# Attention beside a gated feed-forward on one core: the opening reordered, the last even head normalized by transfers, and quarters of output pieces in score bursts

## The chip, the cores and the metric

The kernel runs on one core of one Trainium2 chip. The metric is device time in microseconds (us), from launch to end. The kernel before took 656.79 us (median of three runs, 656.19 to 660.07).

## The reference, cut to what matters

Two branches read the same input `x` (2048 rows of 512) and are mixed row by row with a sigmoid gate. The attention has 32 heads of only 16 columns; the feed-forward has 1376 inner columns and no nonlinearity.

```python
def _A_ref(x, wqkv, wo):                      # H = 32, Dh = 16
    qkv = (x @ wqkv).reshape(B, S, 3, H, Dh).transpose(2, 0, 3, 1, 4)
    scores = einsum("bhqd,bhkd->bhqk", q, k) * (Dh ** -0.5)
    o = einsum("bhqk,bhkd->bhqd", softmax(scores), v)
    return o.transpose(0, 2, 1, 3).reshape(B, S, D) @ wo
def _B_ref(x, w_gate, w_up, w_down):
    return ((x @ w_gate) * (x @ w_up)) @ w_down
g = sigmoid((x * gate_w).sum(-1, keepdims=True))
return g * _A_ref(x, wqkv, wo) + (1 - g) * _B_ref(x, w_gate, w_up, w_down)
```

## The kernel before, in words

**A planner writes the program.** While the kernel is built, a small simulation with an assumed duration for every operation decides the order of the instructions on each engine. Whenever an engine is free and more than one step is possible, `choose` takes the step that the next digit of the string `ORDER` names. What comes out is a fixed list of instructions for each engine, each with the semaphores that it waits for. The assumed durations and latencies (`lat=`, the numbers behind each task, `MM`, `SWITCH`) therefore never run on the chip; they only steer the order.

**Scores.** The queries are cut into 4 chunks of 512 and the heads into 4 blocks of 8, even and odd heads apart: 32 groups. A group has 64 units; a unit is the scores of one head for 128 keys and 512 queries, one matmul (L907) that uses 32 of the 128 rows of the TensorE array. Up to four units, one for each row tile of 32, are issued together as a burst (`burst`). Each unit fills one PSUM bank. There are eight banks: one (`OB`) collects the attention output, and the other seven are shared by score units and by fills.

**Exponentials.** ScalarE takes one or two banks at a time (L968); VectorE takes others with an integer trick (L1002), and GpSimd makes two shifted copies of those (L1051). The products with V (L1100) follow, four column tiles of 32 to a pass.

**Fills.** Everything else on TensorE is a "tile" of four or more pieces, each a pass of four column-tile matmuls (L427): projections `q`, `k`, `v`, the gate `z`, up and gate columns `u` and `g`, and 16 output tiles `o`. An output tile has 15 pieces: 11 with `wd` and the feed-forward's inner result `hT`, and 4 with `wo` and the attention output `OT`. An open tile holds one PSUM bank until its last piece has run.

**Quarters.** The kernel before already holds code by which a burst of fewer than four units takes along a quarter of a fill piece in an empty row tile: 32 of the piece's 128 contraction rows, accumulated into the bank of the tile that the piece belongs to. It is switched off by `Q_KINDS = ""`:

```python
def quarter(js):                              # js: row tiles that the burst's units use
    if len(js) > 3 or not Q_KINDS:
        return None
    tl = parted()                             # a tile one of whose pieces is begun in quarters
    if tl is not None:
        q = next((q for q in tl.quart if q not in js), None)
        return None if q is None else (tl, tl.part, q)
    ...                                       # else the last ready piece of an open tile
```

A piece that is begun in quarters needs all four, one in each row tile, and each quarter waits for the one before it. While its tile has no whole piece left to run, `plan_burst` keeps the row tile of the next quarter free of units (`force`).

**Normalization.** When a group's products are done, VectorE copies them to `oc` (L1192); row 16 (even) or 14 (odd) of each 32 holds the sum of the exponentials. For a pair of groups, transfers bring the sums to `dn` (L1183), VectorE takes reciprocals and multiplies by the gate (L1182, L1180), transfers take the result through DRAM to `rb` (L1179, L1175), and VectorE multiplies `oc` by `rb` into `OT` (L1173). The last pair, groups 30 and 31, goes another way: a float32 matmul with the selector `sel` spreads the sums over the partitions (L1212 for group 30, L1219 for group 31, into one bank), the gate is loaded into `rb` for itself (`tail_even`, L1199), and VectorE does the reciprocals in four parts (L1229, L1232).

**Opening.** Four loads bring the first 512 rows of `x`; TensorE transposes them (L463, copied out by L473 on ScalarE and L475 on VectorE). Matmuls on zeros (L388) fill TensorE before and after. The other rows come by twelve transposing transfers on SyncE's queue. Weights are loaded on SyncE's and ScalarE's queues.

Of the kernel before, what the change touches and what calls it, by code (L numbers as in the profile page):

```python
# [10 lines left out]
F32 = mybir.dt.float32  # L11
I16 = mybir.dt.int16
I32 = mybir.dt.int32
I64 = mybir.dt.int64
# [189 lines left out]
def bass_gated_mix__mha_block__glu_gated_bilinear__prompt_kernel(  # L204
# [15 lines left out]
    "0000000000000001000100000000000000000000100001000000000000202000000024000001000001000000010000100000"  # L220
    "0100003000000001010000000120000200010100000300000100010001000000001010000400000000200000001000500000"
    "0000010000034020100000000000000050000000001000000000120401100000000000000000000000000000000000001011"
    "1000000400000000010000000020000020000300000000000030000000000000000000000000000003000000000000000000"
    "0000200000001000000000100002000000001002100211000001000000200000001000000002000000100000000000000200"
    "0000000000000100000010000002000000000001100011000100000000000100000000000000000000100000050000400000"
    "0000010000000000001010012020000000010000000000000100000000010200000000001102020000000001010000000100"
    "0000000000000000400000000000000000100001000010001000000000001000001000000000000001000000002000000101"
    "1000010000003001000010040000000000000004010000010000101004100000000000000000000001000010100120010000"
    "0000010000000000100400000000000000000001000301000001000000000000050000000100000000000000000000000000"
    "4001010100030000010100002010100000002000000000001000010040000000000000001000000000010100000000000000"  # L230
    "0000000000000000000000000100100000000000000001010001000000000000100001000100000000000000000000001010"
    "0000000000001100000000000000010000020000000000001010101000001000100100041301000001002000000002001000"
    "0000000010000000000040000000001000000000000010000000000000001000000000020000000000000040000011000000"
    "0001000000001000000000001000010000000000200000010000400000010000100000000000000000100000000000000000"
    "0001000000000001000000001000001000000000000000000000100010000014001000000101000000000000000000000000"
    "0000001000010200001000000001000002000000050000000000010210000000020100001000002300000000400004000000"
    "0040000100000000000000000000000000000000000500000000000000000000000004000001100000200000101000000001"
    "0000000000000100010010000000000000000000000000020000200000000000000100000020000000110000100100000001"
    "0000005000000004010000000021010001004000000000020000000000000000000000000000010000000000000000010000"
    "1002000000002000103000000003001000000000400000100200000000000000000010050000000020000000000100000000"  # L240
    "1000001000000004000000000000000000000000000000101000001000001000015000000002000000000130200000010000"
    "0000000000010100000000000000400000001000001000010200000000000000000000001000000001001000100000001010"
    "0000100000020010000100200000004000000000001000100010000000101000020000020000010000400000000000000012"
    "0040000000100030000100000100000040000000000000000010000000000000000000000000000000000050000000000000"
    "0000000000004000001000000000001000000000100100010000010000002000000000100030010000000000001000000400"
    "1000000000001000000001000002000000000000000000000000000000000010000000010010000000000001000000000000"
    "0000000011000000000000000000000000101000000000000001100100000000100000000004010000000010000010000000"
    "0000000100000050000000010010000000200000000000000001010000000011000010020000140010010000000110104000"
    "0000000000120000004000010000040000000000000010000005000000000000002000020000000000000000000000001100"
    "000000000000000000000010000010010000000000000000000000000000000000000"  # L250
# [12 lines left out]
MM, SWITCH, SECOND, MML = 216.0, 106.0, 10.0, 390.0  # L263
# [26 lines left out]
def _build(nc, A_x, A_wqkv, A_wo, W_gate, W_up, W_down, gate_w, out):  # L290
# [8 lines left out]
    with ExitStack() as stack:  # L299
# [32 lines left out]
        sel = sb("sel", [128, 2, 128], F32)  # L332
# [24 lines left out]
        for t in range(4):  # L357
            load(("sp", "act")[t % 2], f"x0{t}", xr[:, t, :], x2[t * 128 : (t + 1) * 128, :], lat=3600)
        load("sp", "wq0", wq[:, :, 0:128], wcol(0, 128), lat=3600)
        load("act", "wk0", wk[:, :, 0:128], wcol(D, D + 128), lat=3600)  # L360
        load("act", "wv", wv, wcol(2 * D, 3 * D), lat=5000)
        t_x = {}
        for ch in range(1, NCH):
            for kt in range(KD):
                load("sp", f"x{ch}{kt}", xT[:, kt, ch * 512 : (ch + 1) * 512],
                     x2[ch * 512 : (ch + 1) * 512, kt * 128 : (kt + 1) * 128], lat=3500, transpose=True)
                K.tasks["sp"][-1][4] = 1330.0
        load("act", "gw", gw[:, :], gate_w.rearrange("(kt p) -> p kt", p=128), lat=6000, prio=7, allow_slow_non_contiguous=True)
        load("act", "wk1", wk[:, :, 128:D], wcol(D + 128, 2 * D), lat=9000, prio=7)
        load("act", "wq1", wq[:, :, 128:D], wcol(128, D), lat=11000, prio=7)  # L370
# [15 lines left out]
        for i in range(11):  # L386
            K.task("pe", lambda: [c["pt0"]] if "pt0" in c else None,
                   lambda pe: pe.matmul(ps[:, OB, :], PT[:, 0, 0:128], PT[:, 0, :], start=True, stop=True), 427.0, 630.0, None, 0,  # L388
                   begun=lambda o: pt_first.append(o), gate=(lambda: not any(tl.name[0] == "x" for tl in tiles)) if i > 8 else None)
# [13 lines left out]
        const("dve", "sl", lambda v: v.memset(sel[:, :, :], -1.0))  # L403
        for j in range(4):
            for p in range(2):
                const("dve", f"sl{j}{p}", lambda v, j=j, p=p: v.memset(sel[:, p, 32 * j + 16 * p : 32 * j + 16 * p + 16], 32.0 * j + 17 - 2 * p), ["sl"], 70, 120)
        const("dve", "sel", lambda v: v.tensor_scalar(sel[:, :, :], sel[:, :, :], io[:, 289:290], None, ALU.is_equal),
              [f"sl{j}{p}" for j in range(4) for p in range(2)] + ["io3"], 330, 400)
# [3 lines left out]
        const("dve", "qz0", lambda v: v.memset(QE[:, :, 1:NB, :], 0.0), (), 1340, 1400)  # L412
# [713 lines left out]
        def finish(m, last):  # L1126
# [8 lines left out]
            def done(o):  # L1135
# [49 lines left out]
                if m == NG - 2:  # L1185
                    tail_even(o)
                if m == NG - 1:
                    tail_odd(last, o)
# [411 lines left out]
```

## Time and profile before

| | |
|---|---|
| median of 3 runs | 656.79 us (656.19 to 660.07) |
| profiled execution | 657.3 us, of which the span from first to last instruction is 655.4 us |
| TensorE matmul busy | 648.9 us (99%) in 8704 matmuls |
| ScalarE busy | 630.3 us (96%) |
| VectorE busy | 594.9 us (91%) |
| GpSimd busy | 543.1 us (83%) |

Matmuls overlap, so the busy time of TensorE is read with the distance from one start to the next. The line numbers are those of the kernel before.

### The profile page before, as it was taken

Reading aid. Unit: us, or ns where it says so; the run is one execution under the profiler, and the core shown is the slowest. Engines: PE = TensorE matmul, PEld = TensorE weight load, DVE = VectorE, ACT = ScalarE, POOL = GpSimd, SP = SyncE. Lnnn points to the kernel's source line nnn. Section 1 sums busy time; section 2 is a strip of 40 time slices with the busy share of each in tenths; the row PEclk is TensorE's granted clock in tenths of the full one; section 3 lists DMA queues with packets and bytes.
Section 4 is the critical chain, followed back from the end, with each engine's and each line's share of the span. In section 5 each row is a group of like instructions: output and inputs, shape, how many; then the busy total and the mean of one; then the engine's idle time right before and its main releaser. Section 6 shows DMA issues by size and latency. Waiting matters only on the chain.

```text
span 655.4 us, 21243 instructions
## 1 busy us (share of the span) xinstructions
PE 648.9 (99%) x8704; PEld 188.4 (29%) x8704; DVE 594.9 (91%) x1006; ACT 630.3 (96%) x808; POOL 543.1 (83%) x1421
## 2 busy tenths in 40 slices
PE   8999999999999999999999999999999999999997
PEld 4332222222222322322223222222223322222223
DVE  7999899999998888999998999999998899999974
ACT  4899999999999999999999999999999999999992
POOL 1569898889879898898988999979897998898780
PEclk9999999999999999999999999999999999999999
DMA  9930201001010100101000010100001010000001
GB/s 177 248 104 7 66 11 36 11 9 30 1 36 10 36 19 15 32 1 36 3 27 20 17 38 10 29 11 9 29 7 41 18 35 3 10 20 2 28 18 36
DMA packets 28531, 21.14 MB, mean 32 GB/s; under 512 B 16360, under 2 KB 24268, under 8 KB 28432
## 3 DMA queue, kind: packets, MB, share of 16 engines
q1 hardware_dynamic: 25504, 18.07, 10.6%
q10 hardware_dynamic: 2928, 1.71, 1.2%
q8 instruction: 68, 1.11, 0.7%
q14 instruction: 31, 0.25, 0.1%
HBM read 11.63 MB, written 2.36 MB: 21 GB/s over the span
## 4 chain that ended last, share of the span: by engine, by line
PE 74%; ACT 21%; DVE 2%; DMA 2%; SPq 1%; issue 0%; DVEq 0%
PE ps L1100 26%; PE ps L907 24%; PE ps L427 23%; ACT PT L968 21%; DVE PT L1002 1%; DMA wq<-in_A_wqkv_dram 1%; DMA oc<-oc 1%; DVE V L553 0%; SPq L522 0%; SPq L1153 0%; PE ps L1212 0%; PE ps L1219 0%; SPq L354 0%; DVE OT L1173 0%; SPq L1175 0%
## 5 line engine op out<-in xcount | busy, mean ns | idle before, releaser
L968 ACT ACTIVATE PT<-ps 128x1024 bf16<-128x1024 f32 (+1 forms) x797 | 623.9, 1011 | 5.3 <-PE ps L907 4.5
L1051 POOL INT64_ADD PT<-PT x1412 | 541.7, 404 | 92.0 <-DVE PT L1002 75.4
L1002 DVE TENSOR_SCALAR PT<-ps 128x512 int16<-128x512 f32 x712 | 463.0, 683 | 39.8 <-PE ps L907 26.4
L907 PE MATMUL ps<-QE,KK 32*128 32x512 bf16 x2048 | 250.6, 384 | 0.9 <-DVE PT L1002 0.7
L1100 PE MATMUL ps<-PT,V 128*32 128x512 bf16 (+1 forms) x2048 | 225.1, 384 | 0.0
L1100 PE MATMUL ps<-PT,VS 128*32 128x512 f16 x1424 | 179.1, 384 | 0.0
L907 PEld LDWEIGHTS ps<-QE,KK 32*128 32x128 bf16 x2048 | 64.3, 90 | 269.4 <-ACT PT L968 202.0
L1100 PEld LDWEIGHTS ps<-PT,V 128*32 128x32 bf16 x2048 | 53.7, 95 | 61.7 <-issue 51.3
L1100 PEld LDWEIGHTS ps<-PT,VS 128*32 128x32 bf16 x1424 | 43.9, 95 | 42.1 <-issue 27.9
L427 PE MATMUL ps<-xT,wu 128*32 128x512 bf16 x704 | 53.7, 383 | 0.0
L427 PE MATMUL ps<-xT,wg 128*32 128x512 bf16 x704 | 52.8, 383 | 0.0
L427 PE MATMUL ps<-wd,wa 128*32 128x512 bf16 x704 | 50.7, 382 | 0.0
L622 DVE TENSOR_TENSOR usb<-ps,omg 128x512 bf16<-128x512 f32 x44 | 30.0, 681 | 1.0 <-PE ps L427 0.9
L649 DVE TENSOR_TENSOR wa<-ps,usb 128x512 bf16<-128x512 f32 x44 | 30.0, 682 | 0.8 <-PE ps L427 0.5
L1192 DVE COPY oc<-ps 128x512 f32<-128x512 f32 x31 | 21.1, 682 | 0.6 <-PE ps L1100 0.5
L427 PE MATMUL ps<-xT,wa 128*32 128x512 bf16 x272 | 20.5, 382 | 0.1
L427 PEld LDWEIGHTS ps<-wd,wa 128*32 128x32 bf16 x704 | 14.9, 95 | 19.8 <-issue 12.3
L427 PE MATMUL ps<-wo,OT 128*32 128x512 bf16 x256 | 20.1, 383 | 0.0
L427 PE MATMUL ps<-xT,wq 128*32 128x512 bf16 x256 | 19.6, 382 | 0.5 <-DMA wq<-in_A_wqkv_dram 0.5
L427 PEld LDWEIGHTS ps<-xT,wg 128*32 128x32 bf16 x704 | 13.8, 95 | 18.2 <-issue 10.6
L427 PEld LDWEIGHTS ps<-xT,wu 128*32 128x32 bf16 x704 | 13.8, 95 | 18.0 <-issue 11.1
L427 PE MATMUL ps<-wa,xT 128*32 128x512 bf16 x256 | 17.6, 381 | 0.0
(74 smaller groups left out, 124.8 us busy)
## 6 DMA issues: line engine op xcount, KB each, us to landing
rb<-rscr SPq DMA_DIRECT2D x15, 256.0 KB
QE<-Qr SPq DMA_DIRECT2D x120, 16.0 KB, 1.8
oc<-oc SPq DMA_DIRECT2D x60, 32.0 KB, 2.0
out_dram<-ost SPq DMA_DIRECT2D x12, 128.0 KB, 2.0
wu<-in_B_w_up_dram SPq DMA_DIRECT2D x1, 1376.0 KB, 7.0
wg<-in_B_w_gate_dram SPq DMA_DIRECT2D x1, 1376.0 KB, 10.8
wd<-in_B_w_down_dram SPq DMA_DIRECT2D x1, 1280.0 KB, 14.2
wa<-in_A_wqkv_dram ACTq DMA_DIRECT2D x1, 512.0 KB, 7.4
```

What stands on the lines that cost most here:

```text
L427: r = pe.matmul(ps[32 * i : 32 * i + 32, bank, :], w, x_, start=s0, stop=s1, tile_position=(0, 32 * i), skip_group_check=True)
L622: return v.tensor_tensor(usb[:, st["s"], :], ps[:, bank, :], omg[:, cf, :], ALU.mult)
L649: return v.tensor_tensor(hT[:, f, :], ps[:, bank, :], usb[:, u_at[cf, f][0], :], ALU.mult)
L907: return lambda pe: pe.matmul(ps[:, bank, :], KK[32 * j : 32 * j + 32, b, kt * 128 : (kt + 1) * 128], QE[32 * j : 32 * j + 32, p, b, :], s ...
L968: o = K.issue("act", lambda a: a.activation(PT[:, cs, :], ps[:, bs, :], ACT.Exp, scale=math.log(2.0) / 1024.0), deps, 51.0 + 427.0 * n, 17 ...
L1002: o = K.issue("dve", lambda v: v.tensor_scalar(PT[:, y, :].bitcast(I16), ps[:, bank, :], BIAS16, 0.0, ALU.add, ALU.max), [dep] + pt_rel[y] ...
L1051: return g.int64_add(PT[:, zl, :].bitcast(I64), PT[:, sl, :].bitcast(I64), w)
L1100: return lambda pe: pe.matmul(ps[32 * it.j : 32 * it.j + 32, OB, :], lhs, it.rhs, start=s0, stop=s1, tile_position=(0, 32 * it.j), skip_gr ...
L1192: K.task("dve", deps, lambda v: v.tensor_copy(oc[:, p, :], ps[:, OB, :]), 600.0, 690.0, done, 0)
```

## The change

It has four parts.

1. **Opening.** Seven matmuls on zeros instead of eleven, five of them ahead of the transposes instead of nine. The load of `wv` goes behind the warm-up of the activation table on ScalarE's queue. `wk1`, `wq1` and `gw` move from ScalarE's queue to SyncE's, behind eight of the twelve transposing transfers. Clearing `QE` and the last rows of `wd` moves from VectorE to GpSimd; the selector is half as wide.
2. **Last even group.** Group 30 is normalized as the groups before it are, over transfers, with the other half of the sums set to 1; the matmul L1212, the gate's load and L1199 are gone. Group 31 keeps its selector matmul; the products of the two are added in four parts behind the four reciprocals, into a buffer that lies over `omg`.
3. **Quarters** are switched on for output tiles (`Q_KINDS = "o"`, at least 4 whole pieces left).
4. **The order.** New assumed durations (`SWITCH`, transposes, latencies of loads) and a new `ORDER` of 3097 digits for the 3069 before, so every stage is ordered anew.

The diff, cut to its core:

```diff
-    "0000000000000001000100000000..."          # ORDER, all digits new
+    "1100110010000010110000000000..."
-MM, SWITCH, SECOND, MML = 216.0, 106.0, 10.0, 390.0
+MM, SWITCH, SECOND, MML = 216.0, 108.0, 10.0, 390.0
-        sel = sb("sel", [128, 2, 128], F32)
+        sel = sb("sel", [128, 128], F32)
-        load("act", "wv", wv, wcol(2 * D, 3 * D), lat=5000)
+        load("act", "wv", wv, wcol(2 * D, 3 * D), lat=5000, prio=7)
         for ch in range(1, NCH):
+            if ch == NCH - 1:
+                load("sp", "wk1", wk[:, :, 128:D], wcol(D + 128, 2 * D), lat=6000)
+                load("sp", "wq1", wq[:, :, 128:D], wcol(128, D), lat=6500)
+                load("sp", "gw", gw[:, :], gate_w.rearrange("(kt p) -> p kt", p=128), lat=6000, allow_slow_non_contiguous=True)
             for kt in range(KD):
                 ...
-        load("act", "gw", ..., lat=6000, prio=7, allow_slow_non_contiguous=True)
-        load("act", "wk1", wk[:, :, 128:D], wcol(D + 128, 2 * D), lat=9000, prio=7)
-        load("act", "wq1", wq[:, :, 128:D], wcol(128, D), lat=11000, prio=7)
-        for i in range(11):
+        for i in range(7):
             K.task("pe", ..., lambda pe: pe.matmul(ps[:, OB, :], PT[:, 0, 0:128], PT[:, 0, :], start=True, stop=True), ...,
-                   gate=(lambda: not any(tl.name[0] == "x" for tl in tiles)) if i > 8 else None)
+                   gate=(lambda: not any(tl.name[0] == "x" for tl in tiles)) if i > 4 else None)
+        const("dve", "dn1", lambda v: v.memset(dn[64:128, NG // 2 - 1, :], 1.0), (), 70, 120)
-        const("dve", "qz0", lambda v: v.memset(QE[:, :, 1:NB, :], 0.0), (), 1340, 1400)
-        const("dve", "wdz", lambda v: v.memset(wd[96:128, FT - 1, :], 0.0))
+        const("pool", "wdz", lambda g: g.memset(wd[96:128, FT - 1, :].bitcast(F32), 0.0), ["wgz"], 320, 350)
+        const("pool", "qz0", lambda g: g.memset(QE[:, :, 1:NB, :].rearrange("p e b n -> p e (b n)").bitcast(F32), 0.0), ["wdz"], 1650, 1700)
 def finish(m, last):                           # in done / dd
-                    if p == 0 or m == NG - 1:
+                    if m == NG - 1 or (p == 0 and m != NG - 2):
                         return
-                    for j in range(4):
+                    for j in range(4 if p else 0):
                 ...                            # reciprocal, rec * gate, two transfers out, one back to rb
+                                    if m == NG - 2:
+                                        K.task("dve", [o, o6, den_op[m], c["eo"]],
+                                               lambda v: v.scalar_tensor_tensor(oc[:, 0, :], oc[:, 0, :], eo[:, 0:1], rb[:, :], ALU.mult, ALU.mult), ...)
+                                        return
-                if m == NG - 2:
-                    tail_even(o)               # gate load, L1199, selector matmul L1212, L1215: all gone
 def tail_odd(...):
-            K.task("pe", ..., lambda pe: pe.matmul(ps[:, tl_["b"], :], sel[:, 1, :], oc[:, 1, :], start=False, stop=True), ...)
+            K.task("pe", ..., lambda pe: pe.matmul(ps[:, tl_["b"], :], sel[:, :], oc[:, 1, :], start=True, stop=True), ...)
             ...                                # rb = oc odd * eo * rb stays
-                   lambda v: v.tensor_tensor(rb[:, :], rb[:, :], oc[:, 0, :], ALU.add)
             for tt in range(4):
-                v.reciprocal(oc[:, 0, q], ps[:, tl_["b"], q])
-                v.tensor_tensor(OT[:, (NCH - 1) % 2, NB - 1, q], oc[:, 0, q], rb[:, q], ALU.mult)
+                v.reciprocal(rq[:, q], ps[:, tl_["b"], q])
+                v.tensor_tensor(rq[:, q], rq[:, q], rb[:, q], ALU.mult)
+                v.tensor_tensor(OT[:, (NCH - 1) % 2, NB - 1, q], rq[:, q], oc[:, 0, q], ALU.add)
-        Q_KINDS, Q_LOOK, Q_MIN, Q_END, Q_CREDIT = "", 3, 2, 60, 54.0
+        Q_KINDS, Q_LOOK, Q_MIN, Q_END, Q_CREDIT = "o", 3, 4, 60, 54.0
```

More of the change, by code (lines that the diff above doesn't have):

```diff
@@ L251 @@
+    "0010001000000000100020000000000002001000000000000010000002001010010000000000000000001000000000101010"
+    "1303000053000200000000020000000003000100000101000110100100000001001001000110000000000000000000000"
 )
@@ L474, in evac @@
                 else:
-                    K.task("dve", [last], lambda v: v.tensor_copy(dst, src), 600.0, 690.0, then, 1, begun=reg)
-            return _Tile(f"x{t}", [piece(kt) for kt in range(KD)], lambda: have([ld.get(f"x0{t}"), c.get("idn")]), evac, -9, "full", 110.0)
+                    K.task("dve", [last], lambda v: v.tensor_copy(dst, src), 440.0, 530.0, then, 1, begun=reg)
+            return _Tile(f"x{t}", [piece(kt) for kt in range(KD)], lambda: have([ld.get(f"x0{t}"), c.get("idn")]), evac, -9, "full", 59.0)
         def mk_k(b, ch, due):
```

127 lines of the change are left out of this document (56 added, 71 removed).

## The prediction

> **What bounds the kernel now.** I read the page's first lines, then the table by stages, then the timeline in one quiet stretch, and last the waits.
>
> ```profile
> PE 648.9 (99%) x8704; PEld 188.4 (29%) x8704; DVE 594.9 (91%) x1006; ACT 630.3 (96%) x808; POOL 543.1 (83%) x1421
> ...
> core 0: us, PE busy (x) PEld busy (x) DVE busy (x) ACT busy (x) POOL busy (x), PEclk, DMA share, GB/s
> 0.00:11.00 11.00, 9.32 (x83) 4.66 (x83) 6.67 (x37) 3.28 (x5) 1.35 (x9) 1.00 0.85 181
> 11.00:40.00 29.00, 28.85 (x434) 9.89 (x430) 28.09 (x52) 26.25 (x42) 16.15 (x42) 1.00 0.97 225
> 160.00:220.00 60.00, 60.00 (x805) 17.07 (x801) 54.77 (x88) 60.00 (x81) 51.66 (x137) 1.00 0.05 14
> ```
>
> Between 11 and 638 us TensorE never stops, and from 40 us on ScalarE's rows leave no gap either; VectorE has about a tenth to spare. Room is in the opening (11 us) and in the tail, from 638 us to the end of the span at 655.4. What TensorE's time is made of shows in the timeline of an output tile, from 205 us:
>
> ```profile
> 205.47 0.39 PE L907 MATMUL ps<-QE,KK 32*128 32x512 bf16 x3
> 205.79 0.61 PE L427 MATMUL ps<-wd,wa 128*32 128x512 bf16 x8
> 206.34 0.39 PE L907 MATMUL ps<-QE,KK 32*128 32x512 bf16 x3
> ...
> 531.27 0.61 PE L427 MATMUL ps<-wo,OT 128*32 128x512 bf16 x8
> ```
>
> A burst starts at 205.47, the first pass behind it at 205.79: 0.32 us. Two passes then take 0.55 us until the next burst, and as the change from passes back to a burst takes about the same 0.32, one pass behind another takes 0.226. So a pass more or less is worth 0.226 us, and a burst more or less (0.87 less two passes) 0.42 us, most of it the two changes between row and column tiles.
>
> ```profile
> 10.82 0.39 PE L907 MATMUL ps<-QE,KK 32*128 32x512 bf16 x4
> 11.14 1.48 PE L427 MATMUL ps<-wa,xT 128*32 128x512 bf16 x24
> ...
> 636.83 0.63 PE L907 MATMUL ps<-QE,KK 32*128 32x512 bf16 x4
> ...
> PEld ps L907 <- ACT PT L968: 202.0, 474, 0.5
> ```
>
> Between the first and the last of these bursts I count 640 for the 2048 units: 153 of four, 468 of three and 19 smaller, so 487 leave a row tile empty. The burst of four at 10.82 is followed after 0.32 us too: a fourth matmul in a burst costs nothing that can be seen. The last line says what keeps bursts small: 474 times the weight load of a burst waited for ScalarE to release a bank. TensorE is busy with earlier passes meanwhile, but banks are what a burst of four lacks.
>
> **Part 1, the opening.** These rows set the first burst (the timeline; then one group of the first 25 us; then three DMA issues, whose last column is the time to landing):
>
> ```profile
> 0.73 0.90 SPq L354 DMA_DIRECT2D PT<-in_A_x_dram  x2
> ...
> 1.18 4.02 PE L388 MATMUL ps<-PT 128*128 128x512 bf16 x9 [1.18 <-DVE small L384]
> 2.69 1.28 ACT L385 ACT_TABLE_LOAD   x1 [2.69 <-issue]
> 4.00 2.05 ACTq L354 DMA_DIRECT2D wq<-in_A_wqkv_dram  x1
> 4.49 1.34 DVE L412 MEMSET QE<- 128x1536 uint32 x1 [0.27 <-issue]
> 5.00 1.91 PE L463 MATMUL ps<-idn,PT 128*128 128x128 bf16 x16
> 6.70 0.69 PE L388 MATMUL ps<-PT 128*128 128x512 bf16 x2
> 6.95 0.60 ACT L473 ACTIVATE xT<-ps 128x512 bf16<-128x512 bf16 x1 [0.25 <-PE ps L463]
> 7.90 1.05 PE L427 MATMUL ps<-xT,wq 128*32 128x512 bf16 x16 [0.50 <-DMA wq<-in_A_wqkv_dram]
> 9.60 0.79 PEld L427 LDWEIGHTS ps<-wa,xT 128*32 128x32 bf16 x20 [0.29 <-DMA wa<-in_A_wqkv_dram]
> ...
> 24.16 1.26 PE L427 MATMUL ps<-wa,xT 128*32 128x512 bf16 x20
> ...
> L907 PE MATMUL ps<-QE,KK 32*128 32x512 bf16 x34 | 3.5, 384 | 0.0
> ...
> wa<-in_A_wqkv_dram ACTq DMA_DIRECT2D x1, 512.0 KB, 7.4
> PT<-in_A_x_dram SPq DMA_DIRECT2D x2, 128.0 KB, 3.0
> wq<-in_A_wqkv_dram SPq DMA_DIRECT2D x1, 128.0 KB, 6.1
> ```
>
> The loads of `x`, issued two by two from 0.73 us, land 3.0 us after issue, the later ones at about 4.2 us, yet the transposes start at 5.00, behind nine matmuls on zeros of 0.427 us each. With five these end at 3.3, and the sixteen transposes (0.107 us apart, 1.7 in all) run from about 3.7 to 5.4 instead of 5.00 to 6.70; the last copy of `xT` ends near 6.0 instead of 7.55. VectorE's clearing of `QE` (1.34 us, in front of its copies) and ScalarE's blocked issue of `wq1` (2.05 us) leave the path too. GpSimd has the clearing hidden: 1.35 us busy in eleven. That is worth up to 1.8 us, if `wq0` comes in time: it landed 6.1 us after issue, shortly before 7.90, and the projection waited 0.50 us for it. Its rivals on the wires then were `wv`, `wk1`, `wq1` and `gw`, all of which now come later; the loads of `x`, of the same size and with few beside them, took 3.0. If it took 6.1 again, the gain would be 0.1. I take 4.4, between the two, by which it lands near 6.0. `wv` is issued some 1.5 us later, behind the table load (1.28), but has fewer beside it; at 9.60 the V passes waited 0.29 for it. At an unchanged 7.4 they could start only 1.5 later than now, at 11.1. The bounds are so -1.8 and +1.5; I take **-1.8**, because the burst at 10.82 needs `wq0` and `wk0` but no V, and the first bursts can run while `wv` lands. The third chunk's four transposing transfers start three issues (about 1.5 us) later; the passes on that chunk came at 24.16 us, when only 34 units were done (the last row but three, for the first 25 us) of the first group's 48 that do without it, so some four bursts cover it.
>
> **Part 2, the last even group.**
>
> ```profile
> 604.47 0.69 DVE L1192 COPY oc<-ps 128x512 f32<-128x512 f32 x1
> 617.91 0.88 DVE L1173 TENSOR_TENSOR OT<-oc,rb 128x512 bf16<-128x512 f32 x1
> 622.90 0.67 DVE L1192 COPY oc<-ps 128x512 f32<-128x512 f32 x1
> ...
> 637.39 0.40 PE L1100 MATMUL ps<-PT,VS 128*32 128x512 f16 x4
> 637.98 1.12 PE L1212 MATMUL ps<-oc,sel 128*128 128x512 f32 x2 [0.20 <-ACT PT L968]
> 639.04 0.83 PE L1100 MATMUL ps<-PT,V 128*32 128x512 bf16 x12
> 640.78 0.60 ACT L1190 ACTIVATE oc<-ps 128x512 f32<-128x512 f32 x1 [0.96 <-PE ps L1100]
> 641.74 1.12 PE L1219 MATMUL ps<-oc,sel 128*128 128x512 f32 x2
> 643.07 1.77 DVE L1229 RECIPROCAL oc<-ps 128x128 f32<-128x128 f32 x2
> 646.77 0.42 DVE L1232 TENSOR_TENSOR OT<-oc,rb 128x128 bf16<-128x128 f32 x2
> 650.80 1.05 PE L427 MATMUL ps<-wo,OT 128*32 128x512 bf16 x16
> 651.91 0.60 ACT L710 ACTIVATE QE<-ps 128x512 bf16<-128x512 f32 x1 [2.67 <-PE ps L427]
> ```
>
> The tail is passes: from 642.8 to the last `wo` pass TensorE doesn't pause. L1212 and the gaps around it hold TensorE from 637.6 to 639.04: 1.4 us in which passes of the last output tiles can run now. The transfers that take its place are off the path. For group 29 copy, sums, reciprocal, two transfers out, one back and the product took from 604.47 to 618.8, 14.3 us; for group 30, from 622.90, that ends near 637, four us before the odd copy (640.78) whose product needs `rb`. If that cover is gone, every us past 641.4 is lost in the odd product. What stays behind the odd copy: VectorE loses one sum of 0.69 and gains four additions of about 0.21 (two products of that size took 0.42), so the last `OT` piece comes near 648 instead of 647.2, still ahead of the last `wo` passes. Bounds 0 and -1.4; I take **-1.4**, as passes are there to fill the hole.
>
> **Part 3, quarters.** The first twelve output tiles run among bursts, from 205 to 531.9 us (the four last ones mostly after the scores, where there are none). Between the first and last piece of each I count 6, 3, 6, 4, 3, 3, 6, 7, 13, 2, 1 and 6 bursts with an empty row tile, 60 in all. Four quarters save a pass. If only whole fours within a tile count, nine passes are saved; if every begun piece is completed in a burst further on, twenty. I take seventeen: 3.8 us less 68 extra matmuls in bursts at 0.004 or less, so **-3.6**. The lower end is not -2 but above nothing, because ScalarE leaves no gap: where TensorE runs ahead, bursts wait for its banks instead, and a shift of work to VectorE costs passes. Bounds -4.5 and, with banks held, +12 (below).
>
> **Part 4, the order.** All choices are new; no row prices this. By the unit price above, twenty bursts fewer or more (3% of 640) are 8.4 us either way. I take 0 and keep both ends.
>
> **The sum.** -1.8 -1.4 -3.6 = -6.8 against the profiled execution: 657.3 - 6.8 = 650.5. The median of the runs shown, 656.79, is 0.5 lower, so the median after would be **650.0**.
>
> **Rivals.**
>
> *The clock stays low in the opening.* The nine matmuls at 1.18 us are 0.427 apart, the passes at 7.90 are 0.216 apart: TensorE ran at half speed until about 6.9, after 5.5 us of work without a pause. With four matmuls fewer there are pauses near 3.5 and 6.2. If full speed comes a few us later, eight passes for Q and K take 0.43 instead of 0.216, 1.7 us, and the opening gains nothing: 651.8. The Trainium skill, "TensorE: Matmul & The Clock Gate", Part 1, speaks for it: full clock comes after a busy window of about 3.4 us in a free-running grid. The trace agrees in that one full window without a pause lies ahead of 6.9; whether a window with pauses counts as busy no row shows.
>
> *ScalarE binds.* It shows no gap in 160 to 220 us. Then passes saved become waits for banks, and only the two ends pay: 656.8 - 3.2 = 653.6. Against it: VectorE has 54.77 of 60.
>
> *Slower: held banks.* An output tile with a begun piece holds one of seven banks until the fourth quarter has found its row tile, and the rule that keeps that row tile free takes a unit out of bursts of four. With 474 bursts already waiting on a bank, bursts of three become bursts of two. If that happens to the 60 bursts of the output windows, thirty more are needed: 30 x 0.42 = +12.6, less the opening and tail: about 666 with no pass saved. Sixteen extra bursts eat up the 6.8. For it: the wait line. Against: an output window is some 6 us long, twelve of them 80 of 655. The Trainium skill, "TensorEngine Tiling (Array Packing)", Restrictions and Gotchas, says the same of row tiling: more pressure on PSUM, as row tiles need banks of their own.
>
> *The new order has fuller bursts.* Fifteen fewer than 640 save another 6.3: 643.7. For it: 487 bursts have room. Against: the same wait line.
>
> **How the numbers follow.** Chances: the forecast, 647 to 653, 0.44 (a little over half of it below 650.2); fuller bursts 0.20; ScalarE binds 0.14; low clock 0.08; held banks 0.14. A measurement of this kernel can tell about 1% from no change, 650.2 to 663.4. Faster by more: 0.25 + 0.20 = 0.45. Slower by more: most of held banks, 0.12. Within: 0.43. The range reaches from 640 to 662.
>
> **What would show it.** Right: the first burst near 9 us; no selector matmul between 637 and 640, and the odd product not waiting for `rb`; matmuls with `wd` or `wo` of 32 rows inside bursts, 60 to 80 of them, and 15 to 20 passes of L427 fewer; about 640 bursts. Wrong: V passes or the third chunk waiting for transfers, passes 0.43 apart after 6.9 us, more than 655 bursts.

## The result, and the profile after

The changed kernel takes **655.39 us** (median of 20 runs, 654.40 to 657.29) against 656.66 us for the kernel before (median of 20, 655.97 to 660.07). The ratio is 0.9979, with a 95% interval of 0.9971 to 0.9987: faster by 1.3 us, where 6.8 were forecast. Measured again beside other kernels, the ratio was 0.9975 (0.9965 to 0.9985).

The profiled execution of the changed kernel (657.29 us, span 655.7) happens to be the longest of its 20. A second profile of the same kernel (`after_again`, 654.47 us, span 652.7) lies at the lower end of its runs; both are read below.

The first lines of the page of the changed kernel, and the table by stages (us, then the busy time and count of each engine, the granted clock, the DMA share and GB/s):

```profile
span 655.7 us, 21110 instructions
...
PE 647.3 (99%) x8690; PEld 187.3 (29%) x8690; DVE 593.0 (90%) x1000; ACT 629.3 (96%) x772; POOL 542.7 (83%) x1397
...
0.00:12.00 12.00, 8.70 (x75) 4.01 (x75) 4.99 (x30) 3.27 (x5) 2.94 (x11) 0.86 0.87 175
160.00:220.00 60.00, 60.00 (x813) 16.90 (x813) 54.99 (x88) 60.00 (x74) 51.40 (x135) 1.00 0.05 14
```

Against the lines of before: TensorE has 1.6 us less to do, ScalarE 1.0, VectorE 1.9. ScalarE still has no gap between 160 and 220 us. New is the clock of 0.86 in the opening, where it was 1.00 (the column counts a drop of the clock; the half speed that both kernels begin with isn't in it).

Where the time went is seen best if both executions are cut at events that both have. The distances below are between starts of instructions in the profiles, except the last two columns, which go from the odd copy's start to the end of the last output tile's copy, and from there to the end of the span. The second profile of the kernel before is the run `before_b`, one execution of 658.21 us.

| us | first burst | to the 200th unit | to the 1000th | to the last unit | to the odd copy | to the last output copy's end | to the end of the span | span |
|---|---|---|---|---|---|---|---|---|
| before | 10.82 | 66.14 | 243.30 | 316.81 | 3.71 | 11.72 | 2.90 | 655.40 |
| before, second profile | 11.33 | 66.26 | 243.54 | 316.81 | 3.71 | 11.72 | 2.90 | 656.26 |
| changed | 12.25 | 66.20 | 243.11 | 316.68 | 3.39 | 10.21 | 3.85 | 655.69 |
| changed, second profile | 10.03 | 65.67 | 243.12 | 316.56 | 3.40 | 10.21 | 3.75 | 652.74 |

The burst stages of one kernel come again to 0.5 us in the first and 0.25 us in the others, the tail to 0.01; what scatters is the opening. From the first row to the last: opening -0.8, the three burst stages -0.9, the tail -0.3 and -1.5, the end +0.85, in all -2.7 us. The medians differ by 1.3 and, in the second measurement, by 2.0; a pair of profiles carries the scatter of two openings. Behind the first burst the two profiles of the kernel before take 644.6 and 644.9 us to the end of the span, the two of the changed kernel 643.4 and 642.7: in the mean 1.7 us less, about as much as the medians differ. So by this estimate the medians hold little or nothing of the opening's -0.8.

**The opening.** First the changed kernel's profiled execution, then its second profile (timeline: start, length, engine, line, what; in brackets the pause ahead and what ended it):

```profile
1.18 2.31 PE L389 MATMUL ps<-PT 128*128 128x512 bf16 x5 [1.18 <-DVE small L385]
2.12 1.28 ACT L386 ACT_TABLE_LOAD   x1 [2.12 <-issue]
2.19 0.47 ACTq L354 DMA_DIRECT2D wa<-in_A_wqkv_dram  x1
3.55 1.59 PE L463 MATMUL ps<-idn,PT 128*128 128x128 bf16 x16
4.98 0.59 PE L389 MATMUL ps<-PT 128*128 128x512 bf16 x2
7.64 1.76 PE L427 MATMUL ps<-xT,wq 128*32 128x512 bf16 x16 [2.07 <-DMA wq<-in_A_wqkv_dram]
9.15 1.96 PE L427 MATMUL ps<-xT,wa 128*32 128x512 bf16 x16
10.86 1.46 PE L427 MATMUL ps<-wa,xT 128*32 128x512 bf16 x20
12.25 0.40 PE L907 MATMUL ps<-QE,KK 32*128 32x512 bf16 x4
...
wq<-in_A_wqkv_dram SPq DMA_DIRECT2D x1, 128.0 KB, 5.8
```

```profile
6.92 1.05 PE L427 MATMUL ps<-xT,wq 128*32 128x512 bf16 x16 [0.80 <-DMA wq<-in_A_wqkv_dram]
8.84 0.77 PEld L427 LDWEIGHTS ps<-wa,xT 128*32 128x32 bf16 x20 [0.50 <-DMA wa<-in_A_wqkv_dram]
8.84 1.26 PE L427 MATMUL ps<-wa,xT 128*32 128x512 bf16 x20
10.03 0.39 PE L907 MATMUL ps<-QE,KK 32*128 32x512 bf16 x4
...
wq<-in_A_wqkv_dram SPq DMA_DIRECT2D x1, 128.0 KB, 5.1
```

The transposes start at 3.55 and 3.81 instead of 5.00 us, near the 3.7 worked out. But the Q projection then waits for `wq0`, which takes 5.8 and 5.1 us to land instead of 6.1: the wait for that transfer grows from 0.50 us to 2.07 and 0.80, and of the 1.45 and 1.19 us gained ahead of it 0.26 and 0.98 reach the Q passes. In the second profile the V passes then wait for `wv` as well (the weight load at 8.84; `wv` landed at 8.79). In the first profile the sixteen Q matmuls also take 1.76 us instead of 1.05: from the second on their passes lie 0.427 us apart, so the clock is at half. The trace's clock records say that it was full from 4.41 to 7.83 us, half from 7.83 to 11.24 and full again after that, and the passes for Q and K fall into the half.

**Bursts and quarters.** The groups of the changed kernel (in all us, mean ns of one | idle before), rows of the list of waits (us, times, longest), and three rows of its timeline in an output window:

```profile
L433 PE MATMUL ps<-wo,OT 32*128 32x512 bf16 x80 | 30.8, 384 | 0.2
L427 PE MATMUL ps<-wo,OT 128*32 128x512 bf16 x176 | 14.3, 382 | 0.0
...
PEld ps L907 <- ACT PT L968: 184.2, 435, 0.5
PEld ps L907 <- issue: 27.8, 67, 0.4
PEld ps L433 <- PE ps L907: 22.2, 54, 0.4
PEld ps L433 <- issue: 9.8, 23, 0.4
...
206.51 0.38 PE L433 MATMUL ps<-wo,OT 32*128 32x512 bf16 x1
206.52 0.39 PE L907 MATMUL ps<-QE,KK 32*128 32x512 bf16 x3
206.84 0.61 PE L427 MATMUL ps<-wd,wa 128*32 128x512 bf16 x8
```

One more row of the waits of the kernel before, and one of `e5_drop` below, in which the order is that of the changed kernel and the quarters are left out (there the scores are L908 and the exponentials L970):

```profile
PEld ps L907 <- issue: 31.8, 76, 0.4
...
PEld ps L908 <- ACT PT L970: 206.1, 487, 0.5
```

The 80 quarters replace 20 passes, all of them with `wo` (176 of 256 `wo` matmuls are left in ordinary passes). A burst with a quarter starts at 206.51 and the pass behind it at 206.84, 0.33 us later, where it was 0.32 without one. But there are 646 bursts now, not 640: 132 of four units instead of 153. In the output windows (204 to 254, 344 to 398 and 485 to 536 us) a burst holds 3.15 units instead of 3.24; elsewhere 3.18 instead of 3.19.

The waits say less than they seem to. The weight loads pause 0.43 us ahead of a burst in the mean whether that is put down to ScalarE (202.0 us in 474 times, before) or to no wait at all (31.8 in 76), so the 474 don't tell how often a bank was missing. And ScalarE's 435 are no fewer waits: in a burst with a quarter, the quarter's load comes first and has the pause to its name (54 and 23 times), and with the quarters left out the row has 487.

**The tail**, in the changed kernel's first profile, and the last row of SyncE's waits:

```profile
622.20 0.68 DVE L1197 COPY oc<-ps 128x512 f32<-128x512 f32 x1
636.16 0.83 DVE L1170 SCALAR_TENSOR_TENSOR oc<-oc,small,rb 128x512 f32<-128x512 f32 x1
639.02 0.83 PE L427 MATMUL ps<-wd,wa 128*32 128x512 bf16 x12
641.63 0.60 ACT L1195 ACTIVATE oc<-ps 128x512 f32<-128x512 f32 x1 [1.69 <-PE ps L1100]
642.59 1.13 PE L1211 MATMUL ps<-oc,sel 128*128 128x512 f32 x2
648.20 0.48 DVE L1223 TENSOR_TENSOR OT<-omg,oc 128x128 bf16<-128x128 f32 x2
650.13 1.05 PE L427 MATMUL ps<-wo,OT 128*32 128x512 bf16 x16
...
SPq L95 <- DMA out_dram<-QE: 2.2, 1, 2.2
```

Group 30 is normalized from 622.20 to 637.0, 14.8 us, and ready 4.6 us before the odd copy. Where L1212 was, passes run (639.02). The selector matmul follows the odd copy's start after 0.96 us as before; from there to the last `wo` passes it is 7.54 us instead of 9.06, because fewer passes of the last output tiles are left: I count 37 that start behind the odd copy, for 44 before. The last wait is longer than before (1.3 us there).

### The profile page after: what moved, and what is told of

Read it like the earlier page. It is cut to its first block, busy times and chain, and to the rows that moved or that the text cites. A ratio compares the mean times of both kernels' runs of the same rounds, so it can differ in the third digit from the quotient of the medians.

```text
span 655.7 us, 21110 instructions
## 1 busy us (share of the span) xinstructions
PE 647.3 (99%) x8690; PEld 187.3 (29%) x8690; DVE 593.0 (90%) x1000; ACT 629.3 (96%) x772; POOL 542.7 (83%) x1397
## 4 chain that ended last, share of the span: by engine, by line
PE 60%; ACT 37%; DVE 1%; DMA 1%; issue 0%; SPq 0%; DVEq 0%
ACT PT L968 37%; PE ps L1100 21%; PE ps L427 20%; PE ps L907 17%; PE ps L433 3%; DVE PT L1002 1%; DMA wq<-in_A_wqkv_dram 1%; DMA gsm<-gscr 0%; PE ps L1211 0%; DVE gsm L592 0%; SPq L354 0%; DVE oc L1197 0%; ACT QE L710 0%; DVE usb L583 0%; DVE rec L1188 0%
## 5 line engine op out<-in xcount | busy, mean ns | idle before, releaser
L907 PE MATMUL ps<-QE,KK 32*128 32x512 bf16 x2048 | 253.5, 384 | 0.1
L1100 PE MATMUL ps<-PT,V 128*32 128x512 bf16 (+1 forms) x2048 | 227.9, 384 | 0.0
L1100 PE MATMUL ps<-PT,VS 128*32 128x512 f16 x1416 | 181.2, 384 | 0.0
L427 PE MATMUL ps<-wd,wa 128*32 128x512 bf16 x704 | 54.5, 382 | 0.0
L433 PE MATMUL ps<-wo,OT 32*128 32x512 bf16 x80 | 30.8, 384 | 0.2
```

The source lines that it names most:

```text
L427: r = pe.matmul(ps[32 * i : 32 * i + 32, bank, :], w, x_, start=s0, stop=s1, tile_position=(0, 32 * i), skip_group_check=True)
L433: return pe.matmul(ps[:, bank, :], lhs[32 * q : 32 * q + 32, :], rhs[32 * q : 32 * q + 32, :], start=s0, stop=s1, tile_position=(32 * q, 0 ...
L907: return lambda pe: pe.matmul(ps[:, bank, :], KK[32 * j : 32 * j + 32, b, kt * 128 : (kt + 1) * 128], QE[32 * j : 32 * j + 32, p, b, :], s ...
L1100: return lambda pe: pe.matmul(ps[32 * it.j : 32 * it.j + 32, OB, :], lhs, it.rhs, start=s0, stop=s1, tile_position=(0, 32 * it.j), skip_gr ...
```

## Experiments

Each kernel is the changed one with the edit shown, except where it says otherwise. Its ratio is against the kernel before, run beside it.

**The changed kernel again** (`after_again`).

> The changed kernel once more, as the yardstick of this series: 655.4 us, 1.3 below the kernel before. Its profile is a second sample of the opening. By the clock theory the pause of 2.1 us ahead of the Q projection falls into one of the clock's windows at another place, so that the passes of Q and K are again 0.427 us apart for some microseconds, or not at all; the first burst lies between 10.6 and 12.3 us accordingly. By the rival, that the pause alone counts and the clock is chance, the first burst stays at 12.2 us.

654.84 us (9 runs), ratio 0.9975 (0.9965 to 0.9985), and the profile shown above. Its Q passes have the full clock, and it is 2.8 us shorter than the first profiled execution: 2.2 in the opening, 0.5 up to the 200th unit. The low clock belongs to some executions of this kernel, not to all.

**Zero matmuls in the pause** (`e1_fill`).

```diff
+        f_ = pt_first[-1].fn                  # the last matmul on zeros, seven times
+        pt_first[-1].fn = lambda pe: [f_(pe) for _ in range(7)][-1]
```

> The changed kernel with six more matmuls on zeros behind the transposes, in the pause ahead of the Q projection; nothing else, and the same order on every engine. Clock theory: TensorE stays busy through the pause, the clock stays at full speed, the passes of Q and K are 0.216 us apart and the first burst comes near 10.7 us instead of 12.2: 1.0 to 1.6 us faster than the changed kernel, about 654.1. Rival, that a later stage paces the kernel whatever the opening does (ScalarE without a gap from 40 us on, or the third chunk of x): the first burst comes earlier but the end doesn't move, 655.4 within 0.4.

655.20 us (9 runs), ratio 0.9976 (0.9966 to 0.9986): no gain over `after_again`. In its profile the pause ahead of Q is nearly filled, the clock stays full, and Q waits for its transfer all the same:

```profile
5.04 1.89 PE L389 MATMUL ps<-PT 128*128 128x512 bf16 x8
7.16 1.05 PE L427 MATMUL ps<-xT,wq 128*32 128x512 bf16 x16 [0.23 <-DMA wq<-in_A_wqkv_dram]
10.19 0.39 PE L907 MATMUL ps<-QE,KK 32*128 32x512 bf16 x4
```

The clock theory falls as the reason for the median. Eight of the profiles here have the opening of the changed kernel as it is. In two of them the clock was low in the passes for Q and K, and these have the longest pauses ahead of Q: 2.07 us (the first profile) and 1.69 us (`e8_act`, where the full clock came for the first time at 10.85 us); with 1.52 us and less it was full.

**`wv` later** (`e2_wv`), **and both** (`e3_both`). The load of `wv` goes behind the first copy of `xT` on ScalarE.

```diff
+        w_ = ld["wv"]
+        P.ops.remove(w_)
+        P.ops.insert(P.ops.index(ev_x[1]) + 1, w_)
```

> The changed kernel with one load moved: wv is issued on ScalarE's queue behind the first copy of xT (about 4.6 us) instead of at 2.2 us. Theory: wq0 took 6.0 us because wv, four times its size, runs on the same wires; without it wq0 lands near 6 us, the pause shrinks to about 0.5 us, the clock stays up and the first burst comes near 9.2 to 9.8 us. The V passes behind K then wait for wv, which lands near 9. About 2 us faster than the changed kernel, 653.4. Rival, that the transposing transfers behind wq0 on its own queue hold it up: wq0 still lands at 7.6, the V passes come later than now, and the kernel is 0 to 1 us slower than the changed one.

> Both edits: six more matmuls on zeros and wv behind the first copy of xT. If each does what its theory says, the fill is mostly hidden behind a pause that has shrunk (six matmuls at full speed are 1.3 us): 653.4 to 654, no better than the moved load alone. If the load's move brings nothing, the fill alone shows: 654.1 to 655. If a later stage paces the kernel: 655.4 within 0.4.

`e2_wv` took 654.76 us (9 runs), ratio 0.9969 (0.9959 to 0.9980); `e3_both` 655.13 (11 runs), 0.9975 (0.9966 to 0.9984). Neither can be told from `after_again`. The profile of `e2_wv`, then the V passes and the first burst of `e3_both`:

```profile
4.61 0.39 ACTq L354 DMA_DIRECT2D wa<-in_A_wqkv_dram  x1
6.20 1.07 PE L427 MATMUL ps<-xT,wq 128*32 128x512 bf16 x16
8.62 1.26 PE L427 MATMUL ps<-wa,xT 128*32 128x512 bf16 x20 [0.49 <-DMA wa<-in_A_wqkv_dram]
9.81 0.39 PE L907 MATMUL ps<-QE,KK 32*128 32x512 bf16 x4
```

```profile
10.29 1.26 PE L427 MATMUL ps<-wa,xT 128*32 128x512 bf16 x20 [1.42 <-DMA wa<-in_A_wqkv_dram]
11.48 0.39 PE L907 MATMUL ps<-QE,KK 32*128 32x512 bf16 x4
```

In `e2_wv` Q starts at 6.20 us, but in the eight profiles with `wv` in its place it starts between 5.72 and 8.01, so that this start alone shows no gain of `wq0`. The transfer itself took 4.2 and 4.0 us in these two runs, for 4.7 to 6.2 in eight of the nine profiles with `wv` in its place (`e1_fill` among them) and 3.7 in the ninth (`e9_hint`): that speaks for `wv` as what slows `wq0`, but two profiles don't show it. Now V waits as well, and TensorE's list has the first V passes ahead of the first burst, as it had in the kernel before (9.62 and 10.82): that burst starts 1.19 us behind the V passes in both runs and in `after_again`. Whatever `wq0` gains, `wv` takes back. The prediction had the first bursts running while `wv` lands; in this list they can't.

**Ordinary passes for the quarters** (`e4_passes`). The quarters are taken out of their bursts; each of the 20 pieces runs as one ordinary pass ahead of the burst that had its last quarter. Order and bursts stay.

```diff
+        for o_, (tl_q, kq_, end_, s1_, d_) in qlog:          # bursts with a quarter
+            o_.parts.pop(0)
+            o_.own = ()
+            if end_:
+                o_.parts.insert(0, (lambda pe, ...: mm_col(pe, tl.bank, tl.pieces[k], False, s1), d_))
```

> The changed kernel, its order on every engine kept, with the quarters undone alone: the 80 quarters are taken out of the bursts, and each of the 20 pieces runs as one ordinary pass of four column tiles ahead of the burst that held its last quarter. Theory, that TensorE binds in the output windows: 20 passes of 0.226 us come back, 4.5 us slower than the changed kernel, about 659.5. Rival, that ScalarE and its banks set the pace there: the passes fall into waiting time, and it is slower by 0 to 1.5 us, 655 to 656.5.

656.55 us (12 runs), ratio 1.0000 (0.9989 to 1.0012). Its stages up to the 1000th and the last unit take 243.88 and 317.64, 0.76 and 1.08 longer than with quarters: 1.84 us for 20 passes, not 4.5. TensorE's list is 4.5 us longer by the unit price (a sum of the nominal distances gives 623.8 for 619.3), but where distances are longer than nominal, the excess shrinks from 9.6 to 7.4 us. And without its quarters the changed kernel is slower in the bursts than the kernel before: the three burst stages take 627.4 us, where before took 626.25 (626.6 in `before_b`), with 729 passes of fills in each. The new order has eight planned bursts more (646 for 638).

**No quarters and no passes for them** (`e5_drop`). The same without the `insert`; the 20 pieces are left out of the sums.

> The changed kernel, its order kept, without the 80 quarters (20 output pieces are left out of the sums, so the output is not the reference's). Theory, that a quarter rides free in a burst: 655.0, within 0.4 of the changed kernel. Rival, that a quarter costs its burst something (its wait for the quarter before it, or a fourth weight load): 80 times 0.01 to 0.02 us, 0.8 to 1.6 us faster than the changed kernel.

654.33 us (5 runs), ratio 0.9961 (0.9946 to 0.9976). Only the last stage changes, 316.06 for 316.56: 80 quarters cost 0.5 us, 0.006 us each. A quarter in an empty row tile is as good as free. Against this run, which has neither, the twenty passes of `e4_passes` cost 2.3 us, 0.12 each: about half of the 0.226 that was their price, the rest falls into time that TensorE would have waited. The 1.84 above is this less the 0.5 of the quarters.

**More for ScalarE** (`e8_act`) **and less** (`e10_cut`). In the output windows, 28 copies of 128 columns stand ahead of exponentials in the one; in the other, 11 exponentials of 1024 columns take only the first half of each of their two banks.

```diff
+            o_.fn = lambda a, g=o_.fn: (a.activation(idn[:], idn[:], ACT.Copy), g(a))[1]           # e8_act
+            o_.fn = lambda a, ...: a.activation(PT[:, cs, 0:256], ps[:, bs, 0:256], ACT.Exp, ...)  # e10_cut
```

> The changed kernel, its order kept, with 28 small ScalarE copies (128 columns, about 0.16 us each, 4.4 us in all) put in front of 28 exponentials spread over the output windows, where the quarters run. It loads ScalarE by about what undoing the quarters loaded TensorE. Theory, that the two engines pace these stretches together, so that a saving on one is half lost in waits for the other: about 2 us slower than the changed kernel (1 to 3), 657. Rival, that TensorE alone binds there: within 0.5 of the changed kernel. Third, that ScalarE alone binds: 4.4 us slower.

> The changed kernel, its order kept, with 11 exponentials of the output windows cut to half their columns on ScalarE (the other half is left out and holds older values, so the output is not the reference's): 4.7 us less ScalarE work where the quarters run. Theory, that both engines pace these stretches: the waits for ScalarE's banks shrink, 1 to 2 us faster than the changed kernel. Rival, that TensorE alone binds: within 0.4. If ScalarE alone binds: 4 to 5 us faster.

Two groups, the first of `e8_act` and the second of `e10_cut`:

```profile
L1463 ACT ACTIVATE idn<-idn 128x128 bf16<-128x128 bf16 x28 | 12.5, 446 | 0.0
```

```profile
L1463 ACT ACTIVATE PT<-ps 128x512 bf16<-128x512 f32 x11 | 7.5, 686 | 0.3 <-PE ps L908 0.3
```

From start to start a copy takes 0.200 us, so 5.6 us are added; an exponential takes 0.904 for 1024 columns and 0.477 for 512, so 4.7 are taken away. `e8_act` took 659.56 us (6 runs; ratio 1.0046, 1.0033 to 1.0060): its stages are 2.07 and 2.82 longer, 4.9 of the 5.6. `e10_cut` took 653.47 us (6 runs; ratio 0.9954, 0.9942 to 0.9966): its stages are 0.42 and 0.73 shorter, 1.15 of the 4.7. So ScalarE has next to no room, and TensorE stands close behind it: 88% of what is added to ScalarE comes through, 52% of what is added to TensorE (2.3 of 4.5, `e4_passes` against `e5_drop`), and 24% of what ScalarE is spared.

**The selector matmul alone** (`e6_tail`). This is the kernel before, with L1212 cut from 512 columns to 2; group 30's heads are then divided by the sums of group 31's.

```diff
-  ... v.memset(sel[:, p, 32 * j + 16 * p : 32 * j + 16 * p + 16], 32.0 * j + 17 - 2 * p) ...
+  ... v.memset(sel[:, p, 32 * j : 32 * j + 32 - 16 * (1 - p)], 32.0 * j + 17 - 2 * p) ...
-  pe.matmul(ps[:, tl_["b"], :], sel[:, 0, :], oc[:, 0, :], start=True, stop=False)          # L1212
+  pe.matmul(ps[:, tl_["b"], 0:2], sel[:, 0, :], oc[:, 0, 0:2], start=True, stop=True)
-  pe.matmul(ps[:, tl_["b"], :], sel[:, 1, :], oc[:, 1, :], start=False, stop=True)          # L1219
+  pe.matmul(ps[:, tl_["b"], :], sel[:, 1, :], oc[:, 1, :], start=True, stop=True)
```

> The kernel before, its order kept, with the selector matmul of the last even group (L1212) cut to two columns; the even heads of the last group are then normalized by their odd neighbours' sums. It prices the removed matmul by itself. Theory, that the tail is passes: 1.0 to 1.4 us faster than the kernel before, about 655.5. Rival, that the matmul stood in a pause in which the last products waited for ScalarE anyway: within 0.4 of the kernel before.

656.21 us (12 runs), ratio 0.9987 (0.9973 to 1.0001).

```profile
637.83 0.63 PE L907 MATMUL ps<-QE,KK 32*128 32x512 bf16 x4
638.99 0.38 PE L1212 MATMUL ps<-oc,sel 128*128 128x2 f32 x2 [0.19 <-ACT PT L968]
639.30 0.83 PE L1100 MATMUL ps<-PT,V 128*32 128x512 bf16 x12
```

From L1212 to the next passes it is now 0.31 us instead of 1.06, and from the last unit to the odd copy 3.23 instead of 3.71: 0.5 us. Behind the odd copy nothing changes (11.74 for 11.72). So the matmul by itself was worth 0.5 us. The other 1.3 of the changed kernel's tail come with what else is ordered anew there: of the passes of fills behind the last unit (46 in both kernels) nine run ahead of the odd copy, for two before, so that seven fewer are left behind it; and six passes of products are left behind the last unit, for eight before. How the 1.3 split between the two was not tried.

**The end** (`e7_branch`, `e9_hint`). Behind the last output copy the changed kernel takes 0.85 us longer. In the DMA view the stretch of the last output transfer shows, for the kernel before (652.4 to 654.4 us) and then for the changed one (651.9 to 655.0):

```profile
q1 hardware_dynamic: 144, 0.13, 19.4%
out_dram<-QE SPq DMA_DIRECT2D x1, 128.0 KB, 1.7
```

```profile
q1 hardware_dynamic: 144, 0.13, 12.9%
q14 instruction: 2, 0.02, 1.3%
out_dram<-QE SPq DMA_DIRECT2D x1, 128.0 KB, 2.6
```

The same 128 KB take 2.6 us instead of 1.7, and two packets of 8 KB on a queue of instructions, fetches of code, fall into that stretch. The packets of the transfer say where the time goes: of its 144, in the changed kernel 135 have ended by 653.40 us, and nine, a sixteenth, end between 653.59 and 654.04. In the three profiles with the old end all 144 end within 0.5 us; in the eleven with the new one five to nine of them end more than 0.5 us behind the middle one. In `e7_branch` VectorE and GpSimd read the flag that decides on their last branch only after the last output; in `e9_hint` ScalarE, VectorE and GpSimd announce that branch 40 instructions ahead.

```diff
-  flag_op + (outs[-1:] if name == "pe" else [])                    # e7_branch
+  flag_op + (outs[-1:] if name in ("pe", "dve", "pool") else [])
-  P.ahead = {"pe": 60, "sp": 250}                                  # e9_hint
+  P.ahead = {"pe": 60, "sp": 250, "act": 40, "dve": 40, "pool": 40}
```

> The changed kernel with one wait more at its very end: VectorE and GpSimd read the flag and branch only after the last output has landed, as TensorE does. Theory: in the changed kernel they branch just ahead of the last output transfer, and the fetch of the code behind the branch (two packets of 8 KB) runs on the same transfer engines, so that the last output lands 2.3 to 2.7 us after its issue instead of 1.7; with the wait it lands after 1.7, and the kernel is 0.6 to 0.9 us faster than the changed one, about 654.3. Rival, that the last landing varies by itself: 655.0 within 0.3; or slower by up to 1 us, if the late fetch itself now ends the kernel.

> The changed kernel with hints for the final branch on ScalarE, VectorE and GpSimd too (40 operations ahead of each one's end), as TensorE and SyncE have them. Theory: the code behind the branch is fetched long before the last output transfer, so that the last output lands about 1.7 us after its issue instead of 2.3 to 2.6: 0.5 to 0.9 us faster than the changed kernel, about 654.4. Rival, that the late landing comes from elsewhere: 655.1 within 0.3.

`e7_branch` took 656.61 us (11 runs), ratio 0.9999 (0.9990 to 1.0008); `e9_hint` 654.80 (12 runs), 0.9980 (0.9970 to 0.9989). In `e7_branch` the last stretch is 3.48 instead of 3.75 us, but the time lies 4.0 us above the span (656.05 and 652.0 in its profile) for 1.7 in `after_again` (654.47 and 652.74): so the program now ends later behind its last instruction, as late fetches would make it; its last two of 8 KB start at 652.86 and 655.25 us, and one is still beside the transfer, at 649.54. In `e9_hint` the fetches still come at 648.88 and 649.48 us, at the time of the last transfer, and the stretch is 3.53. That the end grows by a transfer that takes longer is shown; that the fetches are the reason is likely, but neither run took them all away, and the trace doesn't say which of the 16 DMA engines moved a packet.

## Why the prediction was only partly right

The time lies in the range and the direction was right; of the 6.8 us only 1.3 came in the medians, and 2.7 between two profiles. The terms of the sum one by one:

- **Opening, forecast -1.8.** Between profiles -0.8 (10.82 to 10.03); over the eight profiles with this opening the first burst starts at 10.5 in the mean, against 11.2 in three with the old one; the medians leave it little or nothing, by the estimate above. The transposes moved as worked out. The step that failed is `wq0` landing in 4.4 us: the transfer took 5.8 and 5.1 us in the two profiles, still the last thing that Q waits for. A step ahead of it failed too: `wv` is not issued 1.5 us later, but at 2.19 us, beside the table load of 2.12 us, for 2.12 before. I had put it behind the table load on ScalarE's queue; that load didn't hold up the issue. So the largest rival of `wq0` was on the wires as early as ever; that it is what slows `wq0` isn't shown. A third step, that the first bursts need no V, held for their data but not for TensorE's list, in which the V passes come first.
- **The rival "the clock stays low"** came true in the profiled execution, in another form than I gave: the clock was full from 4.41, earlier than before (6.89), and fell back for 3.41 us when TensorE paused 2.07 us for `wq0`. From the Q passes to the first burst it is 4.61 us there and 2.92 in the four of the eight profiles in which the clock was full and V didn't wait for `wv`: 1.7 us, as priced. Two of eight profiles had it; in `e8_act` it came as I gave it, with the full clock only from 10.85 us. The Trainium skill, "TensorE: Matmul & The Clock Gate", Part 1, has a window of 3413 ns, with which the records agree (3.41), and has the clock fall after an idle window of that length; here a pause of 2.07 us was enough.
- **Last even group, forecast -1.4.** -0.3 and -1.5 in the tail, -1.8 in all. Right in its direction and in what fills the hole, passes. That the size fits is in part luck: the matmul by itself is worth only 0.5 (`e6_tail`), and the rest came with the new order of the last passes and products.
- **Quarters, forecast -3.6.** Twenty passes saved, the upper bound, and quarters nearly free as said (0.006 us each, for 0.004). The failing step is the price: a pass is worth 0.12 us there (2.3 of 20), and 0.09 with its four quarters taken off, not 0.226, since ScalarE sets the pace beside TensorE. In all the quarters gave -1.84. The prediction had the row that says so, 60.00 of 60 us busy, and used it for the lower bound and for a rival alone.
- **Order, forecast 0.** Eight bursts more in the plan, six in the trace; at the same passes it is 1.1 us slower over all three burst stages (`e4_passes`, 627.4 against 626.25; 0.8 against `before_b`). That run keeps the bursts as they were planned around the quarters, so the digits and the rule that keeps row tiles free aren't told apart. With the quarters' gain the bursts win 0.9 between the two profiles.
- **The end, not in the sum.** +0.85: the prediction stopped at the last output copy and took the last transfer as it was.

Put right by these measurements the sum is -0.8 for the opening, -0.9 for the bursts, -1.8 for the tail and +0.85 for the end. Nearest came the rival "ScalarE binds", in which only the two ends pay (653.6): it has the cause, and its -3.2 for the ends was more than the -1.8 that they gave with the last transfer. "Held banks" came in part: bursts in the output windows are emptier (3.15 units for 3.24), but there are 160 of them for 157, and not thirty more. Whether the quarters' rule empties them or the newly drawn order was not tried: with the rule switched off, every later digit of the order would choose among other steps, so that the whole plan would change with it. The wait line that spoke for held banks, and against fuller bursts, was misread: its 474 pauses are as long as those that are put down to no wait.

Of the signs that I named, the 20 fewer passes, the product of group 30 that is ready in time and the passes in place of L1212 were seen; the first burst near 9 us was not, and of the signs against, passes 0.43 apart after 6.9 us were seen in the profiled execution, and V passes waiting for `wv` in the second profile.

## What to carry to other kernels

Where two engines are both over 95% busy, don't price work taken from one at its full length: add a little to each engine and take a little away, and use these shares as the unit price (here 88% for ScalarE and 52% for TensorE added, 24% for ScalarE spared). The stall moved ahead here stopped at the next transfer: before counting a gain in an opening, list what lands next and what else is on the wires, and take its duration from the trace unless a rival really leaves. An end is part of the sum to the last byte landed, and one profile of an opening isn't its median. A pause that is equally long whoever ended it is no wait: compare it with the rows that name nobody before you count it.

## What was not expected of the hardware

- A pause of 2.07 us was followed by 3.41 us of half clock (7.83 to 11.24), after a full clock from 4.41 on. The same opening with pauses of 1.52 us and less kept the full clock.
- A transfer on ScalarE's queue went out at 2.19 us while ScalarE was busy with the table load (2.12 to 3.40).
- The last output of 128 KB took 1.7 us to land with its queue alone, and 2.6 us with fetches of code beside it; nine of its 144 packets came late.
